# Attention, token mixing and gated MLP on one Trainium2 core: for the first batch, the low part of x and the mixing residual are formed by TensorE in PSUM and copied out by ACT

## The chip, the cores and the metric

The program runs on one core of a Trainium2 chip. The metric is the device time of one execution in microseconds (us). The kernel before takes 769.97 us (median of 3 runs, 769.75 to 771.89).

## What is computed

Three stages follow each other, in fp32, for 4 batches of 768 tokens with 512 features. Only the second one and the end of the first are touched by the change.

```python
# 1: chunked attention (8 heads of 64, windows of 64 keys) -> x[b, t, 512]
# 2: token mixing and channel mixing
theta = x @ w_theta
zr, zi = x * cos(theta), x * sin(theta)
y = einsum('ts,bsd->btd', w_tok_r, zr) + einsum('ts,bsd->btd', w_tok_i, zi)
u = x + y
x2 = u + maximum(u @ w_ch, 0)
# 3: x2 @ w_in, gelu, layer norm and token gate w_sg, @ w_out, residual
```

TensorE multiplies in a reduced fp32 format (F32R). To keep the accuracy, each operand is split into a high part (the value rounded to F32R) and a low part (`lo = x - hi`), and each product is three matmuls: hi by hi, hi by lo, lo by hi.

## The kernel before, in words

The first batch's tokens come in six blocks of 128. For each block, attention runs in four steps: `att_s` (scores, row maximum and subtraction on DVE, exp on ACT), `att_t` (TensorE transposes the probabilities, ACT copies them out), `att_v` (product with v, division on DVE, which writes `xt`, 128 tokens by 512) and `att_x`. `att_x` transposes `xt` by four TensorE matmuls with an identity into the one PSUM bank tagged `att` (shared with `att_t`), ACT writes `xhi` from it, and DVE writes `xlo = att - xhi` (the helper `split`, line 113).

`theta` multiplies the block by `w_theta` (12 matmuls of 128x512, line 311, of which the third is the first to read `xlo`), DVE takes the fraction of the angle (`t`, lines 322 and 325), ACT makes sine and cosine (lines 327 to 335), DVE multiplies by x (`z`, line 336), and `z_split` writes its high part on ACT (line 348, tile `slot`) and its two low parts on DVE (line 350). `mix_group` then multiplies z by the token weights (line 378): four accumulators `acc` stay open over the six blocks, 24 matmuls of 128x384 for each block. For the first batch this loop runs twice: over the six blocks for the first half of the output tokens, and again over the stored z for the second half. After the sixth block of a half DVE forms u: `u = acc + xhi` (line 388) and `u = u + xlo` (line 389), and SP's queue sends it to DRAM (line 390). That is eight groups for the first batch and 24 more for the other three.

Beside this run the conversions of the weights from a 64-bit format (`Weights.bits`, lines 150 to 160, and `convert`, lines 203 to 209): one ACT read of the raw words into `cvh`, then on DVE six passes over 128x768 for each token weight (lines 153, 156, 160, 204, 208 and 209), with an ACT rounding (line 203) between. The first six pieces (`convert_pe`, lines 175 to 190) instead let TensorE add and subtract with the identities `id_sb`, `id_neg` (minus identity) and `id_r`, and ACT copies the low part from PSUM. The first half's token weights are converted during the first half, the second half's during the second, together with the second batch's attention.

The order in which an engine issues its instructions is set when the program is built, by a scheduler that works from the order of the calls in `net_kernel`, the dependences and its own costs; each engine then issues in that order and waits where a result is missing. SP issues the loads and the stores of u; the DMA queue of ACT and the POOL engine (GpSimd) take part only in later stages.

## Time and profile before

| | |
|---|---|
| median of 3 runs | 769.97 us (769.75 to 771.89) |
| the profiled execution's own time | 770.49 us |
| its span, first to last instruction | 768.7 us |
| busy: PE / PEld / DVE / ACT / POOL | 95% / 89% / 64% / 40% / 8% |
| mean granted TensorE clock | 0.99 |
| chain that ended last, by engine | PE 65%, DVE 18%, DMA 7%, ACT 6% |

PE is TensorE's matmuls, PEld its weight loads, DVE is VectorE, ACT is ScalarE. L378 is line 378 of the kernel. A matmul's own duration overlaps with its neighbours', so what a run of matmuls costs is read from the distance of their starts. The chain that ended last is followed back from the last instruction, at each step to what released it. Between the span and the execution's own time lie 1.8 us of start and end.

### The profile page before, as it was taken

To read this page: it belongs to the slowest core of one execution; us is meant where nothing else is said; L and a number is where in the kernel's file an instruction comes from. 1 tells how busy PE (TensorE), PEld (TensorE's weight loads), DVE (VectorE), ACT (ScalarE), POOL (GpSimd) and SP (SyncE) were. 2 spreads that over 40 slices of the span, in tenths; PEclk is the share of its full clock that TensorE was granted. 3 is DMA by queue.
4 is the path that set the end of the run, shared out by engine and by line. 5 is a ranking of instruction groups with operands and counts; after the bars stand their busy time and mean duration, and the time that the engine had idled before them with its cause. 6 is when DMAs were issued, how large, how long until landed. Compare 5 with 4: busy or idle time off the path is not lost.

```text
span 768.7 us, 16388 instructions
## 1 busy us (share of the span) xinstructions
PE 732.5 (95%) x6968; PEld 680.8 (89%) x6968; DVE 495.0 (64%) x934; ACT 311.2 (40%) x500; POOL 61.3 (8%) x70
## 2 busy tenths in 40 slices
PE   5979999999999999989998899899999999999998
PEld 3757888999999999989997897899899989998998
DVE  5999898667476665896478958853355435543452
ACT  5965534545545545452124334711151125113310
POOL 0000000000000000160045614200000000000000
PEclk9998999999999999999999999999999999999999
DMA  9775376333233230521077865002100310030002
GB/s 343 283 236 176 134 227 193 111 99 129 95 126 123 84 128 2 205 71 42 28 248 255 285 194 152 10 1 103 62 1 1 109 57 1 1 113 10 1 1 83
DMA packets 35642, 86.92 MB, mean 113 GB/s; under 512 B 4081, under 2 KB 18033, under 8 KB 35569
## 3 DMA queue, kind: packets, MB, share of 16 engines
q1 hardware_dynamic: 30384, 77.22, 29.6%
q10 hardware_dynamic: 5184, 8.65, 4.0%
q8 instruction: 55, 0.90, 0.5%
q14 instruction: 19, 0.15, 0.1%
HBM read 66.98 MB, written 18.87 MB: 112 GB/s over the span
## 4 chain that ended last, share of the span: by engine, by line
PE 65%; DVE 18%; DMA 7%; ACT 6%; issue 3%; POOL 0%; SPq 0%; ACTq 0%; DVEq 0%; POOLq 0%
PE acc L378 16%; PE acc L577 13%; PE acc L597 9%; PE acc L552 8%; PE acc L514 7%; PE th L311 7%; PE att L234 3%; DVE cvh L156 2%; DVE cvm L204 2%; DMA raw<-w_sg 2%; DVE z L336 1%; DMA raw<-w_in 1%; DVE cvm L160 1%; PE att L258 1%; PE att L284 1%
## 5 line engine op out<-in xcount | busy, mean ns | idle before, releaser
L378 PE MATMUL acc<-tok,slot 128*128 128x384 f32 x552 | 116.9, 342 | 2.7 <-ACT slot L348 2.5
L378 PE MATMUL acc<-slot 128*128 128x384 f32 x552 | 115.6, 340 | 0.3 <-DVE u L388 0.3
L378 PEld LDWEIGHTS acc<-tok,slot 128*128 128x128 f32 x552 | 94.5, 188 | 5.2 <-ACT slot L348 2.8
L378 PEld LDWEIGHTS acc<-slot 128*128 128x128 f32 x552 | 95.5, 188 | 2.3 <-DVE u L388 0.6
L577 PE MATMUL acc<-sg_hi,vlo 128*128 128x384 f32 x192 | 64.4, 336 | 0.0
L577 PE MATMUL acc<-sg_hi,vhi 128*128 128x384 f32 x192 | 64.4, 336 | 0.0
L577 PE MATMUL acc<-sg_lo,vhi 128*128 128x384 f32 x192 | 64.4, 336 | 0.0
L311 PE MATMUL th<-th_hi,xhi 128*128 128x256 f32 (+1 forms) x168 | 53.1, 316 | 4.2 <-DVE slot_x L325 2.6
L112 ACT ACTIVATE ghi<-g 128x384 fp32r<-128x384 f32 x32 | 16.8, 525 | 87.7 <-DVE g L586 87.7
L311 PE MATMUL th<-th_hi,xlo 128*128 128x256 f32 (+1 forms) x168 | 51.6, 307 | 0.2 <-DVE xlo L113 0.2
L582 DVE SCALAR_TENSOR_TENSOR g<-acc,g_col,b_bc 128x384 f32<-128x384 f32 x32 | 19.8, 618 | 49.5 <-PE acc L577 49.5
L311 PE MATMUL th<-th_lo,xhi 128*128 128x256 f32 (+1 forms) x168 | 50.8, 302 | 0.0
L432 PE MATMUL acc<-uhi,ch_hi 128*128 128x384 f32 x128 | 44.7, 349 | 5.8 <-DVE x2e L438 5.6
L150 ACT ACTIVATE cvh<-raw 128x256 f32<-128x256 f32 (+1 forms) x44 | 24.8, 564 | 56.6 <-DMA raw<-w_in 19.9
L552 PE MATMUL acc<-x3hi,in_hi 128*128 128x384 f32 x128 | 43.2, 337 | 2.1 <-ACT gu L557 1.3
L432 PE MATMUL acc<-ulo,ch_hi 128*128 128x384 f32 x128 | 44.1, 344 | 0.5 <-DVE ulo L113 0.5
L432 PE MATMUL acc<-uhi,ch_lo 128*128 128x384 f32 x128 | 43.9, 343 | 0.0
L552 PE MATMUL acc<-x3lo,in_hi 128*128 128x384 f32 x128 | 43.0, 336 | 0.0
L552 PE MATMUL acc<-x3hi,in_lo 128*128 128x384 f32 x128 | 43.0, 336 | 0.0
L597 PE MATMUL acc<-glo,out_hi 128*128 128x384 f32 x128 | 43.0, 336 | 0.0
L597 PE MATMUL acc<-ghi,out_lo 128*128 128x384 f32 x128 | 42.9, 335 | 0.0
L597 PE MATMUL acc<-ghi,out_hi 128*128 128x384 f32 x128 | 42.9, 335 | 0.0
(141 smaller groups left out, 1627.5 us busy)
## 6 DMA issues: line engine op xcount, KB each, us to landing
va<-vw SPq DMA_DIRECT2D x24, 520.0 KB, 4.0
ka<-kw SPq DMA_DIRECT2D x24, 512.0 KB, 4.6
raw<-w_tok SPq DMA_DIRECT2D x12, 768.0 KB, 5.7
q<-qt SPq DMA_DIRECT2D x24, 256.0 KB, 3.0
u_dram<-u SPq DMA_DIRECT2D x32, 192.0 KB, 2.2
uf<-u_dram SPq DMA_DIRECT2D x8, 768.0 KB, 6.8
x_dram<-x2e SPq DMA_DIRECT2D x32, 192.0 KB, 3.3
x3f<-x_dram SPq DMA_DIRECT2D x8, 768.0 KB, 4.8
```

The source lines that it names most:

```text
L112: nc.scalar.activation(out=hi, in_=src, func=AF.Copy)
L150: nc.scalar.activation(out=h.bitcast(F32), in_=high.bitcast(F32), func=AF.Copy, scale=REBIAS)
L156: nc.vector.scalar_tensor_tensor(out=h, in0=high, scalar=-0x80000000, in1=h, op0=ALU.bitwise_and, op1=ALU.bitwise_or,)
L234: nc.tensor.matmul(out=out[32 * c:32 * c + 32, j, n * a:n * a + n], lhsT=lhs[h, a, 32 * c:32 * c + 32], rhs=rhs[h, 4 * a + c, :], start=Tr ...
L311: nc.tensor.matmul(out=th, lhsT=a[:, k, tok], rhs=w[:, k, cols], start=(i == 0), stop=(i == 3 * KD - 1),)
L378: nc.tensor.matmul(out=acc[:, 0:TC], lhsT=z[ri][:, zc], rhs=w[:, ri], start=(first and i == 0), stop=(last and i == 5),)
L432: nc.tensor.matmul(out=acc[:, 0:TC], lhsT=w[:, k, ee], rhs=x[:, k, :], start=(i == 0), stop=(i == 3 * KD - 1),)
L514: nc.tensor.matmul(out=acc, lhsT=x[:, k, tt], rhs=w[:, k, :], start=(i == 0), stop=(i == 3 * KD - 1),)
L552: nc.tensor.matmul(out=acc[:, 0:TC], lhsT=w[:, k, ff], rhs=x[:, k, :], start=(i == 0), stop=(i == 3 * KD - 1),)
L577: nc.tensor.matmul(out=acc[:, 0:TC], lhsT=v, rhs=w, start=(i == 0), stop=(i == 3 * NBLK - 1))
L582: nc.vector.scalar_tensor_tensor(out=g, in0=acc[:, 0:TC], scalar=p3["g"][:, f:f + 1], in1=p3["b"][:, tt], op0=ALU.mult, op1=ALU.add,)
L597: nc.tensor.matmul(out=acc[:, 0:TC], lhsT=w[:, k, ee], rhs=x[:, k, :], start=(i == 0), stop=(i == 3 * KD - 1),)
```

## The change

For the first batch alone, `xlo` is no longer formed on DVE. The four transposes of `att_x` open an accumulation group in the bank `att`; ACT writes `xhi` from it as before; then one more TensorE matmul (minus identity by `xhi`, 128x512) is added into the same bank, so that it holds x - xhi, and a second ACT copy writes `xlo`. For the first batch's eight u groups, two matmuls (identity by `xhi`, identity by `xlo`, 128x384 each) are added to the group's accumulator in place of the two DVE additions, one ACT copy writes u, and SP sends it. The identity `id_r` moves to a pool that stays open, because the second half's groups use it after its old pool is closed. Nothing changes for the other three batches.

```diff
-    id_r = stg.tile([128, 128], F32R, name="id_r", bufs=1)
     id_neg = stg.tile([128, 128], F32R, name="id_neg", bufs=1)
+    id_r = const.tile([128, 128], F32R, name="id_r")
...
+        tok = slice(128 * s, 128 * s + 128)
+        early = i < NBLK
         for k in range(KD):
-            nc.tensor.transpose(
-                out=tp[:, 128 * k:128 * k + 128], in_=x[s][:, 128 * k:128 * k + 128], identity=id_sb
+            nc.tensor.matmul(
+                out=tp[:, 128 * k:128 * k + 128], lhsT=x[s][:, 128 * k:128 * k + 128], rhs=id_sb,
+                is_transpose=True, start=(k == 0), stop=(k == KD - 1),
             )
         tp3 = tp.rearrange("p (k t) -> p k t", k=KD)
-        split(xhi[:, :, 128 * s:128 * s + 128], xlo[:, :, 128 * s:128 * s + 128], tp3)
+        if not early:
+            split(xhi[:, :, tok], xlo[:, :, tok], tp3)
+            return
+        nc.scalar.activation(out=xhi[:, :, tok], in_=tp3, func=AF.Copy)
+        nc.tensor.matmul(
+            out=tp3, lhsT=id_neg, rhs=xhi[:, :, tok], start=False, stop=True,
+            skip_group_check=True,
+        )
+        nc.scalar.activation(out=xlo[:, :, tok], in_=tp3, func=AF.Copy)
...
-                    start=(first and i == 0), stop=(last and i == 5),
+                    start=(first and i == 0), stop=(last and i == 5 and b > 0),
...
+            if b == 0:
+                for x in (xhi, xlo):
+                    nc.tensor.matmul(
+                        out=acc[:, 0:TC], lhsT=id_r, rhs=x[:, dt, tt],
+                        start=False, stop=(x is xlo),
+                    )
+                nc.scalar.activation(out=u, in_=acc[:, 0:TC], func=AF.Copy)
+                nc.sync.dma_start(out=u_dram[th][:, dt, :], in_=u)
+        if last and b > 0:
             nc.vector.tensor_tensor(out=u, in0=acc[:, 0:TC], in1=r32(xhi[:, dt, tt]), op=ALU.add)
```

The scheduler also orders the first batch, and its overlap with the second, anew; from about the fourth block of the second batch on (some 170 us into the trace of before), every engine's order is the one of before. Three places matter below. In their rows `xt_118` and `xt_119` are the fifth and the sixth token block, `cvh` and `cvm` a weight conversion's tiles, and the lines of the changed kernel's theta and mixing are 11 higher.

First, DVE ahead of the sixth block's `xt`. Before:

```order
L336 TENSOR_TENSOR z<-z,xt_117 128x1024
L209 TENSOR_TENSOR tok_5_113<-cvh,cvm 128x768
L156 SCALAR_TENSOR_TENSOR cvh<-raw,cvh 128x768
L350 TENSOR_TENSOR slot<-z,slot 128x512
L350 TENSOR_TENSOR slot_x<-z,slot 128x512
L270 TENSOR_SCALAR rs<-att_949 128x8
L160 TENSOR_SCALAR cvm<-cvh 128x768
L273 RECIPROCAL rs<-rs 128x8
L322 TENSOR_SCALAR t<-th 128x512
L274 TENSOR_TENSOR xt_119<-att_949,rs 128x2x4x64
```

and now:

```order
L160 TENSOR_SCALAR cvm<-cvh 128x768
L204 SCALAR_TENSOR_TENSOR cvm<-raw,cvm 128x768
L347 TENSOR_TENSOR z<-z,xt_117 128x1024
L153 TENSOR_SCALAR cvh<-cvh 128x768
L156 SCALAR_TENSOR_TENSOR cvh<-raw,cvh 128x768
L361 TENSOR_TENSOR slot<-z,slot 128x512
L361 TENSOR_TENSOR slot_x<-z,slot 128x512
L270 TENSOR_SCALAR rs<-att_954 128x8
L333 TENSOR_SCALAR t<-th 128x512
L273 RECIPROCAL rs<-rs 128x8
L336 TENSOR_TENSOR t<-th,t 128x512
L274 TENSOR_TENSOR xt_119<-att_954,rs 128x2x4x64
```

A conversion's L204, the next one's L153 and L156, and the second pass of the fifth block's `t` now stand ahead of the sixth `xt`; before, these four came behind it.

Second, DVE behind that `xt`, up to the sixth block's `z`. Before (the second pass of the fifth block's `t` stands between `xt` and the first row):

```order
L204 SCALAR_TENSOR_TENSOR cvm<-raw,cvm 128x768
L113 TENSOR_TENSOR xlo_121<-att,xhi_120 128x4x128
L153 TENSOR_SCALAR cvh<-cvh 128x768
L156 SCALAR_TENSOR_TENSOR cvh<-raw,cvh 128x768
L336 TENSOR_TENSOR z<-z,xt_118 128x1024
L160 TENSOR_SCALAR cvm<-cvh 128x768
L322 TENSOR_SCALAR t<-th 128x512
L204 SCALAR_TENSOR_TENSOR cvm<-raw,cvm 128x768
L350 TENSOR_TENSOR slot<-z,slot 128x512
L350 TENSOR_TENSOR slot_x<-z,slot 128x512
L325 TENSOR_TENSOR t<-th,t 128x512
L336 TENSOR_TENSOR z<-z,xt_119 128x1024
```

and now:

```order
L160 TENSOR_SCALAR cvm<-cvh 128x768
L204 SCALAR_TENSOR_TENSOR cvm<-raw,cvm 128x768
L347 TENSOR_TENSOR z<-z,xt_118 128x1024
L361 TENSOR_TENSOR slot<-z,slot 128x512
L361 TENSOR_TENSOR slot_x<-z,slot 128x512
L333 TENSOR_SCALAR t<-th 128x512
L336 TENSOR_TENSOR t<-th,t 128x512
L347 TENSOR_TENSOR z<-z,xt_119 128x1024
```

The four rows named above and the sixth `xlo` are gone from between the sixth `xt` and the sixth `z`; what remains is in nearly the same order.

Third, ACT around the second block's high part (tile `slot`, L348 before, L359 now). Before, from the load of the sine table:

```order
L327 ACT_TABLE_LOAD
L327 ACTIVATE z<-t 128x512
L329 ACTIVATE z<-t 128x512
L262 ACTIVATE pt<-att 128x512
L335 ACTIVATE z<-z,halfpi 128x512
L203 ACTIVATE tok_2_106<-cvh 128x768
L150 ACTIVATE cvh<-raw 128x768
L348 ACTIVATE slot<-z 128x1024
```

and now:

```order
L203 ACTIVATE tok_2_106<-cvh 128x768
L338 ACT_TABLE_LOAD
L338 ACTIVATE z<-t 128x512
L340 ACTIVATE z<-t 128x512
L262 ACTIVATE pt<-att 128x512
L346 ACTIVATE z<-z,halfpi 128x512
L150 ACTIVATE cvh<-raw 128x768 x2
L359 ACTIVATE slot<-z 128x1024
L203 ACTIVATE tok_3_108<-cvh 128x768
```

The rounding of a token weight (L203) has moved ahead of the load of the sine table, and a second raw read (L150) has moved ahead of the second block's high part.

## Rows read from the trace of the kernel before

**Rows 1.** The page: its span, and part 1 (busy time of each engine).

```profile
span 768.7 us, 16388 instructions
...
PE 732.5 (95%) x6968; PEld 680.8 (89%) x6968; DVE 495.0 (64%) x934; ACT 311.2 (40%) x500; POOL 61.3 (8%) x70
```

**Rows 2.** Stretches: length, busy PE, PEld, DVE, ACT, POOL, granted clock, DMA share, GB/s.

```profile
30.04:55.66 25.62, 21.74 (x409) 17.82 (x409) 23.96 (x40) 19.42 (x26) 0.00 (x0) 1.00 0.75 259
55.66:64.03 8.37, 6.96 (x82) 5.16 (x83) 7.17 (x10) 6.55 (x10) 0.00 (x0) 0.60 0.60 190
...
76.83:89.65 12.82, 11.53 (x118) 9.84 (x118) 10.77 (x16) 6.41 (x10) 0.00 (x0) 1.00 0.36 126
...
94.28:123.30 29.02, 27.24 (x571) 24.30 (x569) 28.47 (x47) 10.79 (x15) 0.00 (x0) 1.00 0.66 204
123.30:139.28 15.98, 15.93 (x336) 14.23 (x337) 12.54 (x28) 8.95 (x13) 0.00 (x0) 1.00 0.52 173
139.28:320.00 180.72, 178.62 (x2550) 167.40 (x2549) 116.72 (x239) 92.26 (x141) 0.00 (x0) 1.00 0.32 101
```

**Rows 3.** Chain that ended last, 74 to 97 us: start, length, engine, tile, line.

```profile
76.24 0.60 DVE xt L274
...
77.43 0.86 DVE cvm L204
...
78.89 0.56 DVE cvh L153
...
79.47 0.96 DVE cvh L156
...
82.04 0.60 DVE t L322
...
85.34 0.63 ACT z L327
...
87.28 1.24 DVE z L336
...
88.54 1.06 ACT slot L348
...
89.65 4.43 PE acc L378 x24
...
94.52 1.05 PE acc L378 x6
```

**Rows 4.** PE in order of time; in brackets its idle time before, and the releaser.

```profile
41.49 1.66 PE L378 MATMUL acc<-tok,slot 128*128 128x384 f32 x8 [1.25 <-ACT slot L348]
...
55.66 0.63 PE L284 MATMUL att<-id_sb,xt 128*128 128x128 f32 x4 [2.24 <-DVE xt L274]
```

**Rows 5.** DVE in order of time, the same columns.

```profile
64.78 0.69 DVE L322 TENSOR_SCALAR t<-th 128x512 f32<-128x512 f32 x1 [1.85 <-PE th L311]
```

**Rows 6.** Instruction groups, 0 to 140 us: count, busy us, mean ns, idle before.

```profile
L150 ACT ACTIVATE cvh<-raw 128x768 f32<-128x768 f32 x12 | 10.9, 905 | 7.3 <-DVE slot L209 5.4 <-DVE tok L209 1.9
...
L113 DVE TENSOR_TENSOR xlo<-att,xhi 128x512 fp32r<-128x512 f32 x8 | 5.5, 686 | 0.5 <-ACT xhi L112 0.3
L112 ACT ACTIVATE xhi<-att 128x512 fp32r<-128x512 f32 x9 | 5.3, 590 | 7.8 <-PE att L284 5.6 <-DVE slot L209 2.2
...
L203 ACT ACTIVATE tok<-cvh 128x768 fp32r<-128x768 f32 x4 | 3.4, 840 | 3.1 <-DVE cvh L156 3.1
...
L388 DVE TENSOR_TENSOR u<-acc,xhi 128x384 f32<-128x384 f32 x8 | 4.4, 551 | 0.2 <-DMA u_dram<-u 0.2
...
L190 ACT ACTIVATE th_lo<-acc 128x512 fp32r<-128x512 f32 x4 | 2.4, 597 | 2.0 <-PE acc L189 2.0
...
L190 ACT ACTIVATE tok<-acc 128x384 fp32r<-128x384 f32 x4 | 1.8, 486 | 0.2 <-PE acc L189 0.2
```

**Rows 7.** The same chain over 0 to 160 us: a theta group, an xlo.

```profile
30.90 3.22 PE th L311 x12
...
59.05 0.61 DVE xlo L113
```

## Prediction

> **What bounds the kernel now.** Start with the page: PE is busy 95% of the span and DVE 64% [rows 1], so over the whole kernel a microsecond of PE work counts and one of DVE work does not. The change adds PE work and takes DVE work away, so everything hangs on the stretch in which it does so. The table of stretches [rows 2] shows that stretch. From 30.04 to 55.66 us DVE is busy 23.96 of 25.62 us, and PE 21.74. From 55.66 to 64.03 us the granted clock is 0.60, a mix of the two levels 1.2 and 2.4 GHz. From 76.83 to 89.65 us PE is idle for 12.82 - 11.53 = 1.29 us. From 94.28 to 123.30 us DVE is busy 28.47 of 29.02 us, and PE 27.24. From 123.30 us on PE is dense (15.93 of 15.98, then 178.62 of 180.72 us), and what is won or lost ahead of it goes through to the end. So the first 123 us are the only place where DVE holds PE up.
>
> What could be won there is PE's idle time: 3.88 us to 55.66; 8.37 - 6.96 = 1.41 us to 64.03; 1.29 us; 1.78 us in the second half [rows 2]. In the slow stretch, 6.96 us of busy time at clock 0.60 are 6.96 x 0.60 = 4.2 us of work at the full clock, so the slow clock itself cost 2.8 us. That makes 11.1 us at the very most. The chain that ended last shows what fills it: from the sixth `xt` at 76.24 us it runs through DVE's conversions (L204, L153, L156), the sixth block's `t`, ACT's sines, `z` and the high part, until PE starts the sixth block's mixing at 89.65 us [rows 3].
>
> **The change, part by part.** PE gains 16 matmuls of 128x384 at 1.05 / 6 = 0.175 us from start to start [rows 3], 2.8 us, and six of 128x512 at 3.22 / 12 = 0.27 us [rows 7], 1.6 us: 4.4 us in all, 1.6 + 1.4 of it in the first half of the output tokens and 1.4 at the end of the second. (The Trainium skill, page "TensorE: Matmul & The Clock Gate", section "Wait — 56ns, not 53.3ns?", gives columns by 2.4 GHz plus 2.5 ns between starts, for bf16. By that the 22 matmuls would be an estimated 16 x 0.1625 + 6 x 0.2158 = 3.9 us, half a microsecond less; the rows here are 8% above it.)
>
> DVE loses six `xlo` at 0.61 us from start to start [rows 7], taken as 0.60, 3.6 us, and eight pairs of additions of 0.551 us each [rows 6], 8.8 us. ACT gains six copies of 128x512 at 0.597 us and eight of 128x384 at 0.486 us, by the copies that `convert_pe` already makes from PSUM [rows 6]: 7.5 us. The first four transposes cost the same as matmuls. SP issues the same eight stores, now after ACT; in its order one load of token weights moves up by one attention load, and the first four stores stand together. I cost this at nothing, since the loads run a block ahead. POOL has nothing here.
>
> *First half, up to the sixth `xt`.* Five `xlo` leave DVE ahead of it: 5 x 0.60 = 3.0 us. But the new order puts four pieces ahead of it that came behind: L204 0.86, L153 0.56, L156 0.96 [rows 3] and a pass over `t` of 0.60, together 2.98 us. The two cancel: `xt` stays where it was, and the gain has to come behind it.
>
> *From the sixth `xt` to the sixth block's mixing*, before: 89.65 - 76.84 = 12.81 us. Now, counted from the end of `xt`: ACT is still in the fifth block's sines (1.94 us from 85.34 to 87.28 [rows 3], begun 0.6 us before the end of `xt`) until 1.3; `xhi` 0.59 [rows 6] until 1.9; PE's subtraction 0.27 and ACT's `xlo` 0.60 until 2.8. Theta's ten matmuls that wait for `xlo`, 2.7, end at 5.5, while ACT writes the fifth block's high part (1.06, until 3.9) and DVE its low parts (1.2, until 5.1). Then `t`, two passes, 1.2; sines 1.94; `z` 1.24; high part 1.06 [rows 3], and about 0.1 of handing over: 11.0. That is 1.8 us less than before, although the way of `xlo` over PE and ACT is longer than DVE's one pass. PE's next mixing starts 1.8 us earlier and then holds eight new matmuls, 1.4 us: at the start of the second half PE is 0.4 us ahead.
>
> *Second half.* DVE loses the first eight additions (4.4 us) just where it is fullest, and PE's 1.78 us of gaps to 123.30 us are waits for DVE's conversions and attention. I take 1.5 of 1.78 as recovered: the four blocks of attention there keep a way over DVE and ACT in which PE waits in order. At its end stand eight more matmuls, 1.4 us. ACT is busy only 10.79 of 29.02 us [rows 2], which hides its copies; without that cover each late copy would hold an accumulator, and so PE.
>
> Sum: -1.8 + 1.4 - 1.5 + 1.4 = **-0.5 us**. The bounds of what is recovered are 0 and 3.6 + 1.85 in the first half (all `xlo`, and DVE's wait of 1.85 us for theta at the slow clock [rows 5]), 0 and 1.78 in the second. Against the profiled execution's 770.49 us this is 770.0; that execution is 0.5 us above the median of 769.97, so the forecast is 769.5 us. A measurement of this kernel can tell about 0.3%, 2.3 us, from no change.
>
> **Rivals.**
>
> *Faster: DVE's relief arrives in full.* DVE is busy 94% of the stretch to 55.66 us, and theta of the fourth block ran at the slow clock after a PE gap of 2.24 us [rows 4]. If the shorter DVE queue closes that gap, the clock stays up, the wait of 1.85 us goes, and the `xlo` time shows: -3.6 - 1.85 + 1.4 - 1.78 + 1.4 = -4.4 us, 765.6 us. Against it: the conversions pulled ahead, and the longer way to `xlo`.
>
> *Slower: ACT and PE hold the second block up.* The new order puts a rounding (0.840 us) ahead of the sine table, and a second raw read (0.905 us [rows 6]) ahead of the second block's high part; `xlo` too is now a link from PE to ACT and back. PE waited 1.25 us for that high part at 41.49 us, and its clock held; it waited 2.24 us at 55.66 us, and the clock fell to 1.2 GHz [rows 2, 4]. If 0.84 + 0.905 come on top of 1.25, the gap is 3.0 us, and a second stretch at the slow clock may follow, worth 2.8 us by the first one, plus some 0.5 us of DVE waiting: -0.5 + 3.3 = +2.8 us, 772.8 us. It decides if PE's gap there reaches the 2.24 us that stood ahead of the fall. Against it: DVE has conversions to work off while it waits, so that a late second block need not delay the sixth `xt`. (A rule that speaks against this change: the Trainium skill, "ScalarE: Activation LUTs", section "Rules for kernel authors", has additions on VectorE and not on ScalarE. The rows do not bear it out for one instruction: 0.486 us for ACT's copy of 128x384 from PSUM, 0.551 us for DVE's addition.)
>
> *Not faster at all: nothing that DVE does here ends on the path.* Then PE pays: +1.4 + 1.4 behind the first half, with no gap closed, +2.8 us, 772.8 us. Against it stands the chain [rows 3], which is DVE's for most of 74 to 89 us.
>
> **How the numbers follow.** Forecast (768.0 to 771.8) 0.61; faster rival 0.22; slower rival 0.12; nothing recovered 0.05. All of the forecast's own range is within 0.3% of 769.97, so that is 0.61 for the same, 0.22 for faster, 0.17 for slower. The range leaves out about half of the faster rival and the outer half of the two slower ones: 766.0 to 772.5 us.
>
> **What would show it.** Right, if the sixth block's mixing starts 1 to 3 us earlier than 89.65 us; if DVE's share in the second half falls below 90% and PE's idle time there is under 0.6 us; if PE's work in the first 140 us grows by 4 to 5 us. The slow clock should show again around the fourth block. The slower rival shows as a stretch at 1.2 GHz before 55 us, with a PE gap over 2.2 us waiting for L359. The faster one shows as a full clock from 30 to 90 us and a mixing of the sixth block before 86 us. The forecast is wrong if the copies of u on ACT are what PE waits for at the start of the second half, or if the later stages differ by over 1 us, where no instruction has changed.

## The result, and the profile after

The changed kernel takes 777.09 us (median of 7 runs, 773.59 to 779.37) where the kernel before takes 770.26 (7 runs, 769.41 to 772.16): a ratio of 1.0081, 95% interval 1.0058 to 1.0104, some 6 us slower. The forecast was 769.5 us, no change; the range ended at 772.5. The profiled execution took 776.21 us, and this is its page:

```profile
span 774.3 us, 16422 instructions
...
PE 734.7 (95%) x6990; PEld 682.4 (88%) x6990; DVE 486.0 (63%) x912; ACT 314.3 (41%) x512; POOL 61.6 (8%) x70
```

Beside [rows 1]: PE does 2.2 us more, DVE 9.0 less (12.4 were counted; added up one by one its instructions take 13.7 us less, so the rest is that they overlap less in the records), ACT 3.1 more (7.5 were counted; two loads of a function table, 1.28 us each, fell away, and again the overlap differs), and the span is 5.6 us longer. To see where, both traces are cut at events that both have: the first `xt`, the start of the second half (first mixing from `slot` alone), and the 21st sine (L327 before, L338 after), from where on both kernels issue the same order. The stretches of the kernel before (columns as in [rows 2]):

```profile
16.99:94.28 77.29, 69.29 (x991) 55.92 (x990) 71.36 (x114) 54.08 (x73) 0.00 (x0) 0.96 0.62 215
94.28:231.57 137.29, 134.22 (x2249) 122.95 (x2247) 101.46 (x197) 66.19 (x99) 0.00 (x0) 1.00 0.43 139
```

and of the changed kernel, with some that answer to [rows 2]:

```profile
17.15:96.63 79.48, 71.38 (x1004) 57.72 (x1004) 69.45 (x106) 57.89 (x82) 0.00 (x0) 0.98 0.59 208
96.63:236.95 140.32, 136.29 (x2258) 124.27 (x2257) 95.06 (x182) 65.84 (x103) 0.00 (x0) 1.00 0.41 135
...
30.74:58.37 27.63, 22.25 (x411) 18.25 (x411) 25.47 (x41) 22.49 (x30) 0.00 (x0) 1.00 0.71 243
58.37:63.00 4.63, 4.63 (x76) 3.35 (x77) 3.72 (x6) 3.73 (x7) 0.00 (x0) 0.66 0.66 230
79.06:90.59 11.53, 10.71 (x116) 9.14 (x114) 7.26 (x11) 6.40 (x11) 0.00 (x0) 1.00 0.21 70
96.63:125.65 29.02, 27.02 (x628) 23.95 (x627) 25.54 (x42) 11.27 (x17) 0.00 (x0) 1.00 0.69 223
```

The first part is 2.19 us longer, the second 3.03; all that follows adds 0.22 (537.13 us before, 537.35 after). In the first part PE's idle time is what it was: 77.29 - 69.29 = 8.0 us before, 79.48 - 71.38 = 8.1 after. DVE was relieved, and PE waited as long as before. In the second part PE's idle time even grows, from 3.07 to 4.03 us. The copies on ACT came out as forecast (groups by form, columns as in [rows 6]):

```profile
L203 ACT ACTIVATE slot<-cvh 128x768 fp32r<-128x768 f32 x6 | 4.9, 840 | 6.6 <-PE acc L389 6.6
L405 ACT ACTIVATE u<-acc 128x384 f32<-128x384 f32 x8 | 3.8, 486 | 3.9 <-DMA u_dram<-u 2.6 <-PE acc L401 1.3
L299 ACT ACTIVATE xlo<-att 128x512 fp32r<-128x512 f32 x6 | 3.6, 593 | 1.3 <-PE att L295 1.2
```

The copies took 0.486 and 0.593 us (0.486 and 0.597 forecast). The first row's 6.6 us, in which ACT's rounding of the second half's weights waits for PE's mixing, explains nothing by itself: that group waited 5.7 us before, and it waits the same 6.6 us in the first experiment below, which does not have the loss. PE's waits in order of time (columns as in [rows 4]):

```profile
44.33 1.49 PE L389 MATMUL acc<-tok,slot 128*128 128x384 f32 x7 [2.30 <-ACT slot L359]
...
58.37 0.63 PE L286 MATMUL att<-id_sb,xt 128*128 128x128 f32 x4 [2.37 <-DVE xt L274]
...
90.59 2.18 PE L389 MATMUL acc<-tok,slot 128*128 128x384 f32 x11 [0.81 <-ACT slot L359]
```

The wait ahead of the second block's mixing grew from 1.25 us [rows 4] to 2.30, the one ahead of the fourth block's transposes stayed (2.24, now 2.37), and the sixth mixing starts at 90.59 us instead of 89.65 [rows 3].

### The profile page after: what moved, and what is told of

Same layout as the page of the kernel before. It is cut to its first block, busy times and chain, and to the rows that moved or that the text cites. A ratio compares the mean times of both kernels' runs of the same rounds, so it can differ in the third digit from the quotient of the medians.

```text
span 774.3 us, 16422 instructions
## 1 busy us (share of the span) xinstructions
PE 734.7 (95%) x6990; PEld 682.4 (88%) x6990; DVE 486.0 (63%) x912; ACT 314.3 (41%) x512; POOL 61.6 (8%) x70
## 4 chain that ended last, share of the span: by engine, by line
PE 66%; DVE 17%; DMA 8%; ACT 6%; issue 3%; POOL 0%; ACTq 0%; SPq 0%; DVEq 0%; POOLq 0%
PE acc L389 16%; PE acc L597 13%; PE acc L617 9%; PE acc L572 8%; PE th L322 7%; PE acc L534 7%; DMA x_dram<-x2e 3%; PE att L234 3%; DVE cvh L156 2%; DMA raw<-w_in 2%; DVE cvm L204 2%; DVE cvm L160 1%; PE att L286 1%; PE att L258 1%; DVE z L347 1%
## 5 line engine op out<-in xcount | busy, mean ns | idle before, releaser
L150 ACT ACTIVATE cvh<-raw 128x256 f32<-128x256 f32 (+1 forms) x44 | 24.7, 563 | 53.0 <-DMA raw<-w_in 20.3
```

The lines of the kernel that those rows point to most:

```text
L150: nc.scalar.activation(out=h.bitcast(F32), in_=high.bitcast(F32), func=AF.Copy, scale=REBIAS)
```

## The experiments

The question is whether the loss is the price of the new instructions or the **order** in which the scheduler issues everything else once they are there. So the first experiment takes the order back. In all tables below, "6th xt" and "2nd half" are us from the first `xt`, "2nd part" is from the start of the second half to the 21st sine, all in the profiled execution; the ratio is to runs of the kernel before on the same chip.

| kernel | 6th xt | 2nd half | 2nd part | median us (before) | ratio (95%) |
|---|---|---|---|---|---|
| before | 59.17 | 77.29 | 137.29 | | 1 |
| the change | 61.31 | 79.48 | 140.32 | 777.09 (770.26) | 1.0081 (1.0058 to 1.0104) |
| order before, all | 59.21 | 79.46 | 137.27 | 772.83 (772.11) | 1.0017 (0.9995 to 1.0038) |
| low part only | 60.89 | 77.30 | 137.53 | 772.40 (772.11) | 1.0016 (0.9992 to 1.0040) |
| sums only | 58.78 | 78.31 | 140.97 | 777.17 (772.11) | 1.0070 (1.0044 to 1.0095) |
| four sums of 2nd half only | 59.48 | 77.61 | 138.75 | 772.54 (772.11) | 1.0005 (0.9985 to 1.0026) |

**The order held.** A helper at the end of `net_kernel` ties the common instructions of an engine into a chain, by tables of their numbers; the added ones stand between as the scheduler puts them.

```diff
+    def pin(engine, spans):
...
+        order = [mine[n] for a, b in spans for n in range(a, b)]
+        for first, then in zip(order, order[1:]):
+            tc.add_manual_dep(
+                then, first.name,
...
+    pin(mybir.EngineType.DVE, [
...
+    pin(mybir.EngineType.Activation, [
...
+    pin(mybir.EngineType.PE, [
...
```

> The change in full, but every instruction that both kernels have is issued on DVE, ACT and TensorE in the order of the kernel before; the added ones stand between. Seen in the traces: of the change's 5.5 us, 2.8 are the 16 added identity matmuls (start of the second half and its end), 0.94 lie ahead of the sixth block's mixing, 1.75 are more idle TensorE time in the second half. Theory ORDER (the loss beyond the 2.8 us is the scheduler's new order, conversions one after the other and work pulled ahead of the attention): 770.3 + 2.8 less the two gains that the prediction counted (1.8 and 1.5) = 769 to 771, mixing of the sixth block no later than 89.7 us. Theory ROUND TRIP (the low part now goes transpose, ACT, TensorE, ACT over one att bank, and the scores behind it wait): it stays at 775 to 778 whatever the order. Theory TENSORE WORK (only the 22 added matmuls count, 4.4 us of TensorE): 774 to 775.

Measured 1.0017: most of the loss is gone, with all 22 matmuls and 14 copies still there. That refutes ROUND TRIP as the whole cause, and TENSORE WORK (4.4 us would be 1.0057). ORDER's own forecast came out in part only: 772.83 us is 0.7 above the kernel before on that chip, and the sixth mixing started at 90.31 us, not by 89.7. Its stretches:

```profile
16.88:96.34 79.46, 71.66 (x1004) 57.55 (x1004) 69.02 (x106) 58.51 (x82) 0.00 (x0) 0.98 0.62 211
96.34:233.61 137.27, 135.09 (x2260) 124.72 (x2259) 93.93 (x182) 68.29 (x105) 0.00 (x0) 1.00 0.43 136
```

The second part is back to 137.27 us although PE carries eight more matmuls there; its idle time fell from 3.07 to 2.18. The first part is as long as in the change. So the order explains the second part, and something else, or something more, the first.

**The parts alone.** Low part only (the sums as before), sums only, and four of the eight sums:

```diff
-            if b == 0:
+            if False:
...
-        early = i < NBLK
+        early = False
...
-            if b == 0:
+            if b == 0 and th == 1:
```

> Only the low part of x is made by TensorE and ACT (six matmuls, six ACT copies); the sums of u stay on DVE as before. ROUND TRIP: most of the 5.5 us less 2.8 is here, 772.5 to 774. ORDER: depends on what the scheduler makes of it, between 768.5 and 773. TENSORE WORK: 1.6 us more, 771.5 to 772.

> Only the sums of u are made by TensorE (16 identity matmuls) and copied out by ACT; the low part stays on DVE. ROUND TRIP: nothing of it is left, 2.8 us of matmuls less up to 1.5 us of idle time won back, 770.5 to 773. ORDER: between 769.5 and 775. TENSORE WORK: 2.8 us more, 773.

> Only the four sums of the second half of the tokens go to TensorE and ACT (8 matmuls, 4 copies); all else as before. Every theory has 1.4 us of matmuls at the end of the second half, where TensorE is 98 percent busy: TENSORE WORK and ROUND TRIP 771.7. ORDER: as this edit moves few instructions (DVE keeps its order but for the sums), 771 to 772; below 770.3 would say that the DVE time set free at 139 us is worth more than the matmuls.

The low part alone costs nothing that this measurement can tell; the sums alone carry the loss (+1.02 and +3.68 us, of which the first is less than the 1.4 us of the eight matmuls in it). With only the last four sums the second part grows by 1.46, which is 8 x 0.175 = 1.4 us of matmuls, as a plain price would be. So it is with the first four off DVE, at the start of the second half, that the scheduler's other order comes.

**Which order in the second half.** The same chains from the first attention of the second half on (all three engines, then one at a time), or in the first half alone:

```diff
+    pin(mybir.EngineType.DVE, [
+        (122, 124), (127, 128), (138, 139), (128, 129), (124, 125), (129, 130), (125, 126), (130, 131),
...
```

> The change in full; only from the first attention of the second half on (DVE), from the first L150 of it (ACT) and from its first mixing matmul (TensorE) the common instructions keep the order of the kernel before. Measured from the first xt to the start of the second half, and from there to the 21st sine behind it, the traces so far read: before 77.29 and 137.29 us, the change +2.19 and +3.03, the change in the order before +2.17 and -0.02, the sums alone +1.02 and +3.68. ORDER IN THE SECOND HALF (3 us of the loss are the order in which the second half's conversions and attention are issued): first part about +2.2 as in the change, second part 0 to +0.5, in all 2 to 3 us faster than the change, ratio to before 1.002 to 1.005. Rival, PRICE (the second part's +3.0 is the added matmuls and what the copies on ACT hold up): second part stays at +2.5 to +3.5, ratio 1.007 to 1.009.

> The change in full; only up to the sixth block's xt the common instructions keep the order of the kernel before, the rest is left to the scheduler. ORDER IN THE SECOND HALF: the second part keeps most of its loss, +2 to +4 us against before; ratio 1.005 to 1.009. First part: sixth xt 59.2 us behind the first (before 59.17, the change 61.31); the start of the second half is then +0.8 to +2.2. Rival (the first half's order sets what follows): second part near 0, ratio 1.002.

> The change in full, only DVE's order of the second half held as in the kernel before (from its first attention on); ACT and TensorE are left to the scheduler. Second part (start of the second half to the 21st sine behind it): before 137.29, the change +3.03, all three engines held -0.03. If DVE's order (conversions in pairs, two in work at a time) carries the loss: -0.5 to +0.7. If it is ACT's (L203 of the next conversion behind the exponentials instead of ahead of them, two of three such places are put back by DVE's order): +1 to +2. If TensorE's: +2.5 to +3.5.

> The change in full, only ACT's order of the second half held as in the kernel before (from its first L150 on); DVE and TensorE are left to the scheduler. If DVE's order carries the loss: +2.5 to +3.5 in the second part. If ACT's: -0.5 to +0.7.

> The change in full, only TensorE's order of the second half held as in the kernel before. Second part: the change +3.03 us, DVE's order held +1.65, ACT's +2.80, all three -0.03. If TensorE's order carries what DVE's does not, +1.0 to +2.0; if it carries all and DVE follows it, -0.5 to +0.7; if it is nothing without DVE's, +2.5 to +3.5.

| held | 2nd half | 2nd part | median us (before) | ratio (95%) |
|---|---|---|---|---|
| 2nd half, all three | 82.16 | 137.26 | 773.85 (771.43) | 1.0036 (1.0017 to 1.0056) |
| 1st half, all three | 79.67 | 142.53 | 778.90 (771.43) | 1.0101 (1.0079 to 1.0122) |
| 2nd half, DVE | 79.10 | 138.94 | 776.46 (771.15) | 1.0066 (1.0045 to 1.0087) |
| 2nd half, ACT | 82.12 | 140.09 | 776.80 (771.15) | 1.0063 (1.0043 to 1.0084) |
| 2nd half, TensorE | 82.13 | 138.10 | 776.01 (771.28) | 1.0064 (1.0038 to 1.0089) |

Holding the second half takes the whole 3.03 us out of the second part; holding the first half leaves it in, and more (in that trace the granted clock is 0.57 from 108 to 112 us, a slow stretch that the others do not have there). That run's sixth `xt` came 60.43 us behind the first, not 59.2. Of the single engines TensorE's order gives back 2.2 of 3.03, DVE's 1.4, ACT's 0.2. DVE's +1.65 lay where its expectation had named ACT, and ACT's +2.80 rules that out; TensorE's +0.81 lay in none of its ranges. So no engine's order carries the loss alone. Part of what differs is seen on DVE (columns as in [rows 5]). In the change one conversion ends every 7.1 us, L209 behind L209, and a new one begins only then:

```profile
105.94 0.96 DVE L209 TENSOR_TENSOR slot<-cvh,cvm 128x768 fp32r<-128x768 f32 x1
...
108.14 0.55 DVE L153 TENSOR_SCALAR cvh<-cvh 128x768 int32<-128x768 int32 x1
...
113.08 0.96 DVE L209 TENSOR_TENSOR slot<-cvh,cvm 128x768 fp32r<-128x768 f32 x1
...
115.28 0.55 DVE L153 TENSOR_SCALAR cvh<-cvh 128x768 int32<-128x768 int32 x1
...
120.21 0.96 DVE L209 TENSOR_TENSOR slot<-cvh,cvm 128x768 fp32r<-128x768 f32 x1
```

With the order held they run in pairs: the second one's L156 stands ahead of the first one's L209, and two end within 4.4 us:

```profile
105.24 0.95 DVE L156 SCALAR_TENSOR_TENSOR cvh<-raw,cvh 128x768 int32<-128x768 int32 x1
106.11 0.95 DVE L209 TENSOR_TENSOR slot<-cvh,cvm 128x768 fp32r<-128x768 f32 x1
...
110.49 0.96 DVE L209 TENSOR_TENSOR slot<-cvh,cvm 128x768 fp32r<-128x768 f32 x1
...
117.25 0.95 DVE L156 SCALAR_TENSOR_TENSOR cvh<-raw,cvh 128x768 int32<-128x768 int32 x1
118.11 0.95 DVE L209 TENSOR_TENSOR slot<-cvh,cvm 128x768 fp32r<-128x768 f32 x1
```

On ACT, in the change, L203 stands behind the exponential of the same cycle and waits there for PE:

```profile
108.31 0.63 ACT L251 ACTIVATE p<-p 128x512 f32<-128x512 f32 x1 [0.50 <-DVE p L247]
110.61 0.85 ACT L203 ACTIVATE slot<-cvh 128x768 fp32r<-128x768 f32 x1 [1.66 <-PE acc L389]
```

and with the order held L203 stands ahead of it:

```profile
108.23 0.85 ACT L203 ACTIVATE slot<-cvh 128x768 fp32r<-128x768 f32 x1 [0.23 <-PE acc L389]
108.99 0.61 ACT L251 ACTIVATE p<-p 128x512 f32<-128x512 f32 x1
```

Two conversions are in work in both orders (in the change the second one's first passes stand ahead of the L209 at 105.94); what differs is how soon all four are through. Counted from the start of the second half the fourth L209 starts at 27.3 us before, at 30.4 in the change and at 26.2 with the order held; with TensorE's order alone at 27.4, with DVE's at 27.5, with ACT's at 30.7. The loss in the second part goes with it roughly: 0.81, 1.65 and 2.80 us in the last three. Between its passes on DVE each conversion needs ACT's L203, and that waits for PE's mixing, so DVE's pairs are one way to quicken this round and TensorE's order another: there each L209 comes 5 to 8 us behind the last. Which instruction of TensorE's order does it stays open.

**The way of the low part over TensorE.** With all orders held (as in the first experiment), the sixth block's low part left on DVE; one DVE instruction of the tail moved; the low part over TensorE for blocks 3 to 5 only; and that with only the first half's four sums.

```diff
-        early = i < NBLK
+        early = i < NBLK - 1
...
-        early = i < NBLK
+        early = 2 <= i < NBLK - 1
...
-            if b == 0:
+            if b == 0 and th == 0:
```

For the second of them, in DVE's table:

```diff
-        (85, 86), (87, 88), (111, 112), (116, 118), (88, 89), (118, 119), (97, 98), (119, 120), (95, 97),
-        (98, 100), (114, 116), (106, 108), (112, 114), (120, 124), (127, 128), (138, 139), (128, 129),
+        (85, 86), (87, 88), (111, 112), (116, 118), (88, 89), (118, 119), (97, 99), (119, 120), (95, 97),
+        (99, 100), (114, 116), (106, 108), (112, 114), (120, 124), (127, 128), (138, 139), (128, 129),
```

> As the change in the order before, but the sixth block's low part stays on DVE, so that its TensorE subtraction and ACT copy fall away ahead of the twelve theta matmuls that the sixth mixing waits for. In the order before, the change's sixth theta starts 2.60 us behind the end of its xt, 0.62 later than in the kernel before, and the sixth mixing is 0.77 us later. TENSORE QUEUE (the subtraction stands on TensorE ahead of theta and costs its time there): the sixth mixing 72.7 us behind the first xt, 0.6 to 0.8 earlier than with all six; in all 0.7 us less than the change in the order before. Rival (the work that DVE is rid of is worth more than the subtraction): no earlier, or later by up to 0.6 as DVE gets its 0.60 back.

> As the change in the order before, with one instruction moved on DVE: the second operation of the sixth block's t (L336) directly behind its first (L333), ahead of L204 and two slot subtractions, which stood between them for 2.0 us in the order before. If the sixth mixing waits for the sines behind t (chain of waits), TensorE's 1.13 us of waiting ahead of it goes: the sixth mixing 72.2 to 72.5 us behind the first xt (73.43 without the move), in all 1 us less. If the freed DVE time is not on the path, or the fifth block's slot subtractions that are now later hold TensorE up instead, no change.

> As the change in the order before, but the low part goes over TensorE for the third, fourth and fifth block alone; the first, second and sixth stay on DVE. From xt to xt, with all six over TensorE and the order held, the stretches behind the first and second block take 0.53 and 0.70 us longer than before, behind the third 0.20, and the fourth's is 0.9 to 1.3 shorter. ROUND TRIP (TensorE and ACT hold the next block's scores up by more than DVE gains): the first two stretches return to 11.65 and 13.58, the start of the second half lies 77.3 + 1.4 less 0.5 to 1.0 = 77.7 to 78.3 behind the first xt (79.46 with six), in all 1 to 1.5 us less than that kernel, ratio to before 1.000 to 1.002. Rival (what DVE is rid of counts): the second half starts no earlier than with five blocks, 79.3 or later.

> As the run with blocks 3 to 5, and of the sums only the four of the first half go to TensorE and ACT; the four of the second half stay on DVE, which idles there. The second half loses the 8 matmuls at its end (1.4 us) and keeps what DVE's relief at its start gave: second part -1.4 to -1.8 against before, first part +0.5 to +1.0, in all -0.5 to -1.3: 769.5 to 771 where before has 771 to 772, ratio 0.998 to 1.000. Rival (the sums on DVE at the end of the second half are on the path): second part -0.4 to 0, ratio 1.001.

| kernel | 6th xt | 2nd half | 2nd part | median us (before) | ratio (95%) |
|---|---|---|---|---|---|
| 6th on DVE | 59.57 | 79.29 | 136.91 | 774.48 (771.43) | 1.0037 (1.0021 to 1.0053) |
| tail, t first | 58.92 | 79.13 | 136.80 | 774.24 (771.43) | 1.0036 (1.0018 to 1.0054) |
| blocks 3 to 5 | 58.82 | 78.54 | 136.91 | 770.99 (771.15) | 1.0004 (0.9986 to 1.0022) |
| blocks 3 to 5, four sums | 58.62 | 78.35 | 136.54 | 771.68 (771.15) | 1.0000 (0.9981 to 1.0020) |

With all six, held in order, the second block's `xt` comes 12.17 us behind the first, the third 14.28 behind the second (before 11.65 and 13.58). With blocks 3 to 5 only these are 11.67 and 13.56 again: the two early blocks paid 0.5 and 0.7 us. The reason stands on PE and DVE of the kernel with all six. PE:

```profile
31.20 0.50 PE L295 MATMUL att<-xhi,id_neg 128*128 128x512 f32 x1 [0.22 <-ACT xhi L294]
31.63 0.45 PE L234 MATMUL att<-ka,q 64*32 64x64 f32 x30
```

and DVE:

```profile
32.20 0.69 DVE L245 TENSOR_REDUCE mx<-att 128x8 f32<-128x512 f32 x1 [1.24 <-PE att L234]
```

The subtraction waits for ACT's `xhi` in the middle of the next block's scores, and DVE waits for those: the 0.60 us that DVE no longer spends on `xlo` it spends waiting. In the kernel before the same instruction waits for nothing:

```profile
31.39 0.68 DVE L245 TENSOR_REDUCE mx<-att 128x8 f32<-128x512 f32 x1
```

Over the five `mx` between the first and the sixth `xt` this wait adds up to 1.9 us, where it was 0.0.

Most of the expectations were missed. With the sixth block on DVE the sixth mixing came 73.26 us behind the first `xt` (72.7 expected, 73.43 without), and no time was won that the runs can tell. Moving `t` in the tail brought nothing (from the sixth `xt` to the second half 20.21 us, 20.25 without): PE's wait ahead of the sixth mixing shrank from 1.13 to 0.85 us, but that mixing started later, 74.11 us behind the first `xt`. The run does not tell whether `t` was off the path or whether the slot subtractions, now later, cost what it gave. With blocks 3 to 5 the second half came at 78.54 (77.7 to 78.3 expected), with a ratio inside the forecast. The four sums less saved 0.37 us of the 1.4 expected, so the price of 1.4 us found above does not hold in every order.

**The second block, and the clock.** In the runs of the low part alone the medians hide two groups: six of twelve at a mean granted clock of 0.987 to 0.991 (median 775.1 us), six at 0.995 to 0.998 (770.5). The kernel that held the second half alone shows a fall of the clock in its trace. Its wait on PE ahead of the second mixing:

```profile
47.49 1.49 PE L389 MATMUL acc<-tok,slot 128*128 128x384 f32 x7 [2.29 <-ACT slot L359]
```

and the 5 us behind it (clock: third figure from the right):

```profile
47.49:52.49 5.00, 5.00 (x80) 4.51 (x81) 5.00 (x10) 1.45 (x2) 0.00 (x0) 0.67 0.39 135
```

The granted clock is 0.67, a mix of the levels of 1.2 and 2.4 GHz. In the profiled execution of the change, with its wait of 2.30 us at the same place, the same 5 us read:

```profile
44.33:49.33 5.00, 5.00 (x85) 4.03 (x86) 5.00 (x10) 2.34 (x4) 0.00 (x0) 1.00 0.41 133
```

Where the clock fell, the second half started at 82.16 instead of 79.48 us. But of these 2.7 us, 1.06 were lost before the fall, between the first and the second `xt` (13.25 us, 12.19 in the change). There PE was slower in the run with the fall. The same two matmuls of a weight conversion, in the change and in that run:

```profile
15.90 1.12 PE L184 MATMUL acc<-cvh,id_th 128*128 128x512 f32 x2
```

```profile
17.98 2.07 PE L184 MATMUL acc<-cvh,id_th 128*128 128x512 f32 x2
```

That leaves 1.6 us behind the fall. To see what the wait is worth, eleven instructions of the second block on ACT were held as before (sines ahead of L203, high part ahead of the second L150), first with the low part alone, then with the change in full and the second half held:

```diff
+    pin(mybir.EngineType.Activation, [
+        (31, 32), (37, 39), (32, 34), (39, 40), (34, 35), (50, 51), (59, 60), (40, 41), (68, 69),
+    ])
```

> The low part alone over TensorE, as in the run of that part, with eleven ACT instructions of the second block held in the order before: its sines ahead of the rounding L203, its high part L359 ahead of the second read L150. With the scheduler's order TensorE waits 2.55 us for L359 ahead of the second mixing (1.25 before), and the runs of that kernel fall in two groups: six of twelve with a mean granted clock of 0.987 to 0.991 and a median of 775.1 us, six of 0.995 to 0.998 with 770.5 us. GAP (ACT's order makes the wait, and the wait brings the half clock): the wait is 1.2 to 1.5 us, no run has a clock under 0.992, the median is 770 to 772. Rival (the clock falls for another reason): a third or more of the runs still have a clock of 0.991 or less.

> The change in full with the same eleven ACT instructions held in the first half, and the second half held on all three engines (as in the run that held the second half alone, 773.85 us, three of twelve runs at a clock of 0.991 or less). GAP: no run has a clock under 0.992, 772 to 773.5 us, ratio to before 1.001 to 1.003. Rival: the same clocks as there, ratio 1.003 to 1.005.

| kernel | 6th xt | 2nd half | 2nd part | median us (before) | ratio (95%) |
|---|---|---|---|---|---|
| low part, second block held | 58.36 | 75.92 | 137.82 | 770.72 (771.28) | 0.9994 (0.9975 to 1.0012) |
| full, both places held | 58.41 | 77.37 | 137.04 | 769.89 (771.28) | 0.9993 (0.9972 to 1.0015) |

The wait is 1.25 us again, and no run of either kernel has a mean clock under 0.995. The full change, with its order held in these two places, is no slower than the kernel before; 769.89 us is less than the 772 to 773.5 expected. But the eleven are not all that moved. With them tied the scheduler ordered the rest of the first half anew: at least 28 of its 122 DVE instructions stand elsewhere than in the change, and 19 elsewhere than in the kernel before. In this third order the wait ahead of the fourth block fell too, from 2.37 to 1.18 us, and the second pass of the fifth block's `t` is behind the sixth `xt` again. So the runs show that the same instructions in another order cost nothing that can be told; they do not show that the wait ahead of the second block was the cause.

**What is left as a gain.** The low part over TensorE, sums on DVE, both places held (the change in full less the sums); the same with the first two blocks on DVE; and the kernel before, without any of the change, in the order of the first of these.

```diff
-        early = i < NBLK
+        early = 2 <= i < NBLK
```

> The low part of all six blocks over TensorE, the sums on DVE as before; the eleven ACT instructions of the second block and the second half on all three engines held as before. With the eleven held, the start of the second half lay 75.92 us behind the first xt (before 77.29), and the clock stayed at 1.00; with the second half held, its second part was between -0.02 and -0.38 against before. Sum: -1.4 + 0 to -0.4 = -1.4 to -1.8 us, ratio 0.997 to 0.9995. If the first half's gain is that of one execution, ratio 1.000.

> As the run before, with the low part of the first two blocks left on DVE, where the way over TensorE cost 0.53 and 0.55 to 0.70 us. ROUND TRIP: another 1.0 us less, the second half starts 74.8 to 75.2 us behind the first xt, ratio 0.996 to 0.999. Rival: DVE misses the 1.2 us ahead of the fourth block's xt, TensorE's wait there is again 2.2 us as before and the clock falls: 77 us, ratio 0.999 to 1.001.

> Nothing of the change: the kernel before, its DVE, ACT and TensorE instructions issued in the order of the run with the low part of all six blocks (the six low parts on DVE, where their inputs allow). If the gain there is the order's (TensorE's wait ahead of the fourth block under 2 us, clock up), the second half starts 75.9 to 76.6 us behind the first xt and the ratio is 0.997 to 0.9995 here too. If it is DVE's relief, the clock falls at the fourth block as before and the second half starts at 77 to 77.6 us, ratio 1.000.

| kernel | 6th xt | 2nd half | 2nd part | median us (before) | ratio (95%) |
|---|---|---|---|---|---|
| low part, both places held | 58.37 | 75.93 | 137.60 | 768.02 (771.89) | 0.9953 (0.9937 to 0.9969) |
| blocks 3 to 6 | 58.84 | 76.38 | 137.73 | 769.92 (771.89) | 0.9964 (0.9946 to 0.9981) |
| before, in that order | 59.98 | 77.64 | 138.21 | 772.30 (771.89) | 1.0003 (0.9983 to 1.0022) |

The low part in that order is faster than the kernel before by more than the measurement's 0.3%, and by more than expected (0.997 to 0.9995). Its waits on PE at the two places, and the stretch that holds the fourth block:

```profile
42.99 1.66 PE L389 MATMUL acc<-tok,slot 128*128 128x384 f32 x8 [1.26 <-ACT slot L359]
...
56.31 0.63 PE L286 MATMUL att<-id_sb,xt 128*128 128x128 f32 x4 [1.18 <-DVE xt L274]
```

```profile
56.31:64.00 7.69, 7.13 (x96) 5.80 (x96) 7.69 (x11) 7.46 (x11) 0.00 (x0) 1.00 0.70 247
```

The wait ahead of the fourth block is halved (2.24 us before), and the clock, 0.60 there before [rows 2], is 1.00. The order does that without the relief too. The kernel before in that order:

```profile
58.44 0.63 PE L284 MATMUL att<-id_sb,xt 128*128 128x128 f32 x4 [1.35 <-DVE xt L274]
```

```profile
58.44:66.00 7.56, 6.73 (x93) 5.09 (x94) 7.56 (x11) 6.21 (x10) 0.00 (x0) 1.00 0.73 243
```

Its clock fell later instead, to 0.72 from 72 to 78 us, and its time is that of the kernel before: 1.0003. Its expectation named the two readings by wait and clock and by time, and the result is split between them. The relief in the scheduler's own order gave no time either: 1.0016. Both together are faster than the order alone.

How much of the gain is the relief's is open. In the traces the first part is 1.36 us shorter than before and the second 0.31 longer, 1.05 in all. Another 2.7 us of the two profiled executions' difference lies behind the 21st sine (537.13 us before, 534.43 here), where no order differs and where the trace of before has two slow stretches:

```profile
409.00:413.00 4.00, 3.54 (x13) 3.06 (x12) 4.00 (x8) 1.43 (x3) 2.48 (x3) 0.58 0.81 278
432.00:437.00 5.00, 4.05 (x15) 4.08 (x16) 4.93 (x13) 1.20 (x3) 3.18 (x4) 0.66 0.56 177
```

The run with the second block alone held has the same first half, instruction by instruction, and a second part only 0.22 us longer, yet its ratio is 0.9994 (twelve runs on another chip; here six). Nothing on record tells where the difference of 0.4% comes from.

Leaving the first two blocks on DVE was a miss. The second half started at 76.38 us, later than with all six (75.93) and not at 74.8 to 75.2. Their `xt` did come as before (11.66 and 13.58 us apart), but the fourth stretch took 13.26 us (11.75 with all six), because in this execution the clock fell at the fourth block, behind the same wait of 1.18 us:

```profile
56.83 0.63 PE L286 MATMUL att<-id_sb,xt 128*128 128x128 f32 x4 [1.18 <-DVE xt L274]
```

```profile
56.83:64.50 7.67, 7.11 (x87) 5.37 (x88) 6.52 (x9) 6.47 (x11) 0.00 (x0) 0.78 0.74 258
```

## Why the prediction was wrong

**Prices: right but for one.** The matmuls of the sums (0.174 to 0.18 us from start to start, 0.175 forecast) and the copies on ACT came as costed, and the four sums of the second half alone cost 1.46 us (1.4 forecast). The six subtractions took 0.34 to 0.66 us to the next matmul's start, 0.42 on average, where 0.27 was forecast; and the prediction's remark that the rows are 8% above the estimate beside them holds for the matmuls of 128x384 alone, since its own 0.27 and 0.2158 us for the others are 25% apart. The copies of u on ACT are not what PE waits for: with the order held they are all there, and PE idles less than before. (The Trainium skill, "ScalarE: Activation LUTs", section "Rules for kernel authors", has additions on VectorE and not on ScalarE. The rows here do not test that: ACT only copies, in 0.486 us, against 0.551 [rows 6] for DVE's addition, and the adding is TensorE's.)

**The first half's step failed.** "`xt` stays where it was, and the gain has to come behind it": the sixth `xt` came 2.14 us later, counted from the first. The step added up DVE's passes ahead of it, 3.0 against 2.98, as if DVE's busy time set the pace. The four pieces pulled ahead cost what was said: the last stretch, from the fifth to the sixth `xt`, took 10.97 us instead of 8.69, 2.28 more, and 2.98 less one `xlo` is 2.38. What did not come is the relief. The first three stretches took 0.53, 1.57 and 0.45 us longer; only the fourth was shorter, by 2.68, and there the clock was low for some 3.4 us instead of 6.8. Even with the order held the sixth `xt` came no earlier (59.21 us, before 59.17): in the first two blocks the freed time went into DVE's wait for scores (0.70 and 1.24 us), because the next block's scores on PE wait for the subtraction and this for ACT's `xhi`. The prediction had counted the 1.6 us of the six subtractions, but its sum holds none of them ahead of the sixth `xt`, and nothing for this way round. Behind `xt` the tail shortened, 79.06 to 90.59 = 11.53 us (11.0 forecast, 12.81 before), but from a start 2.2 us too late. Of the 2.19 us of the first part, 2.09 are PE's busy time, and only 0.1 is idle time.

**The second half's step failed.** "I take 1.5 of 1.78 as recovered": with the order before, the second part lost nothing although it holds 1.4 us of new matmuls, so about 1.4 was recovered (PE's idle time shrank by 0.9 of it); in the scheduler's order the part was 3.03 us longer instead. The forecast for the second half was -1.5 + 1.4 = -0.1 us. The prediction looked at what the new order pulled ahead of the sixth `xt` and took the second half's order as unchanged. There the new order is the loss: with it taken back on all three engines the 3.03 us are gone. The second half's weights are converted later in it (the fourth is through at 30.4 instead of 27.3 us), in a round of DVE, ACT and PE; of the single engines TensorE's order counts for most, and DVE's pairs alone do not explain it.

**The slower rival was half of it.** Both pieces that it named stand ahead of the second block's high part, and the wait (2.30 us) passed the 2.24 us that it set as the point of decision. But in the profiled execution of the change the clock held at 1.00 behind it, so that the 2.24 us decided nothing; and where the clock did fall what was lost behind the fall is 1.6 us (2.8 forecast). It got 0.12; the order had shown both pieces already, and only the clock was uncertain. Its sum, +2.8 us, is half of the loss and knows nothing of the second half.

**What of the sum holds.** In the full change with both places held, the first part is 0.08 us longer than before and the second 0.25 shorter, and the ratio is 0.9993: 0.5 us less, the forecast's own sum. That is luck: the terms came in otherwise, and the interval (0.9972 to 1.0015) holds anything from -2.2 to +1.2 us. The faster rival's mechanism (a shorter gap and the clock up at the fourth block) appears with the low part alone, but in another order, and the first part is then 1.36 us shorter, not 5.45. That the median there is 3.9 us less, near the rival's 4.4, is no confirmation: only 1.05 us of it is found in the part that was changed.

**The tests stated.** DVE's share in the second half fell to 25.54 / 29.02 = 88%, under 90%: right. PE's idle time there is 2.00 us, not under 0.6; the sixth mixing is 0.94 later, not 1 to 3 earlier: both wrong. PE's busy time grew by 2.09 + 2.07 = 4.2 us to the 21st sine, inside the 4 to 5 forecast, but not by the terms counted, 1.6 + 1.4 and 1.4 (it also depends on how long the clock is slow). The slow clock showed at the fourth block (0.66). Later stages differ by 0.2 us in these two executions; over the profiled executions of all the kernels here, which share that order, they are up to 3.4 us shorter than in the trace of before.

Open: why the scheduler gives up the pairs when four sums leave DVE, what in TensorE's order costs the most, and how the 2.2 us of the first part divide between the order, the new matmuls and the clock; the runs show only what the choice costs in all.

## What to carry to other kernels

Where a scheduler sets the order, taking work off an engine also reorders what stays: hold the old order for one run before calling a price a price, then free it in pieces; and look at what the scheduler does with the pieces left free, which may move as well. Time freed on an engine that takes turns with others in a round can become waiting there, as it did here in the first two blocks. A change that loses as a whole may hold a part that wins: here its low part, with two places of the order held, at 0.9953, though its traces account for only about a third of that. One trace of each kernel is one execution: a difference is laid to a change only where the two traces are alike up to that place.

## What had not been expected of the hardware

A wait of PE does not by itself decide what its clock does next. At the second block the same wait of 2.29 or 2.30 us was followed by 5 us at a granted clock of 0.66 or 0.67 in three profiled executions (the second half held on all engines, on ACT, on TensorE) and by 1.00 in two (the change; the second half held on DVE), and a wait of 2.55 us by 1.00 in the low part alone. PE's instructions ahead of it stand in the same order in the first five, but they did not run alike: in the three with the fall PE still took 2.07 us for the two L184 matmuls at some 18 us, in the others 1.12, and the second `xt` came 13.25 us behind the first instead of 12.2. So the fall went with what PE had done before, in all six; whether that is its cause, or chance, the runs do not tell. The granted clock in the profile reads 1.00 in both cases at that early place.

At the fourth block the clock fell behind each of the 15 waits of 1.95 us or more, and behind one of the five of 1.35 us or less: 1.18 us was followed by 1.00 in three profiled executions and by 0.78 in one.

Over all runs, 23 of the 56 of the six kernels with a wait of 2.29 us or more at the second block had a mean clock of 0.991 or less, and none of the 42 runs of the kernels with the eleven instructions held. That is a loose sign, since the mean clock sums up every slow stretch: two of the three profiled executions with the fall have 0.993, and two kernels with a wait of 1.25 and 1.27 us there (the first half held; `t` first in the tail) have four runs of 18 at 0.991.
